# Hash attention: the bits of a pair made one whole pair ahead, and GpSimd's indirect DMAs put in front of its bit DMAs

## The chip, the cores and the metric

The kernel runs on one core of one Trainium2 chip. The metric is the device time of one execution in microseconds (us). Before the change it is 787.45 us, the median of three runs (785.88 to 792.85). The engines are named as in the profile: PE multiplies matrices and PEld loads its weights, DVE is the vector engine, ACT the scalar engine (it computes the exponentials), POOL is GpSimd, and SP issues most DMAs. Each engine runs its own list of instructions in order; a DMA is issued by one of SP, ACT or POOL, in that engine's order.

## The reference

Two parts follow each other. The first is attention in which a query sees only the keys of its own bucket; the bucket is made of the signs of six projections. With B = 4, H = 8, S = 768 and D = 64 there are 32 heads. The second is a mixer: an MLP over tokens and an MLP over channels.

```python
def _attn_ref(q, k, v, proj) -> np.ndarray:
    B, H, S, D = q.shape
    scale = 1.0 / np.sqrt(D)
    n_bits = proj.shape[1]
    q_bits = (np.einsum('bhsd,dk->bhsk', q, proj) > 0).astype(np.int64)
    k_bits = (np.einsum('bhsd,dk->bhsk', k, proj) > 0).astype(np.int64)
    powers = 2 ** np.arange(n_bits)
    q_bucket = np.sum(q_bits * powers, axis=-1)
    k_bucket = np.sum(k_bits * powers, axis=-1)
    mask = q_bucket[:, :, :, None] == k_bucket[:, :, None, :]
    scores = scale * np.matmul(q, k.transpose(0, 1, 3, 2))
    scores = np.where(mask, scores, -1000000000.0)
    scores = scores - np.max(scores, axis=-1, keepdims=True)
    attn = np.exp(scores)
    attn = attn / (np.sum(attn, axis=-1, keepdims=True) + 1e-09)
    return np.matmul(attn, v).astype(np.float32)
...
def _moe_ref(x, w_tok1, w_tok2, w_ch1, w_ch2) -> np.ndarray:
    xt = x.transpose(0, 2, 1)
    h = np.maximum(xt @ w_tok1, 0.0) @ w_tok2
    u = x + h.transpose(0, 2, 1)
    h2 = np.maximum(u @ w_ch1, 0.0) @ w_ch2
    return (u + h2).astype(np.float32)
```

## The kernel before

Two heads make a pair, so there are 16 pairs. Fourteen of them ("regular", `NREG = 14`, the loop `for n in range(NREG)` at L998 to L1061) compute whole 768 x 768 score matrices, with the bucket comparison added as a product of bits: a row of signs of the queries times a row of large values of the keys. The other two ("sorted", `class Sorted`, pairs 14 and 15) put queries and keys into tables ordered by bucket and compute only blocks within a bucket; their work is spread over the iterations of the regular pairs. After the attention, from about 304 us on, the two MLPs run; they are not touched.

One iteration of the loop handles regular pair n. On PE it holds, in order:

- the scores of pair n (`scores`, L484 to L518): 12 blocks of 128 keys by 384 queries for two heads. Each block is a product of bits (`sc<-bits`) and two products of q and k (`sc<-qk`), all at L501. ACT turns each block into exponentials (`exps<-sc`, L412), DVE adds them up (`esd`, L448 to L457).
- the sums of the pair before (`sums`, L534), and the projection of the next pair's q and k, `Hash` (L348 and L353), both into one PSUM tile called `hash`
- the weighing of pair n (`weigh`, L468) in two halves, exponentials times v into `acc`. ACT moves each half out as `num` (L477 and L478).

PSUM is handed out as a ring of four tiles with the tag "sc" (`bank_pair`, L269): a score block, the `hash` tile and the `acc` tile each take the next one, and a tile is taken anew only when its last reader has finished. A late reader of any of the four so holds up PE some blocks on.

`Hash.spread` (L358 to L377) makes the bits: two DVE comparisons (L364 for k, L365 for q) write signs into a corner of `XT`, and 16 small DMAs copy them into one of two tiles, `bitrows[n % 2]` (names `bits_119` and `bits_120` in the order of instructions): eight for k, of which SP issues six and ACT two, and eight for q, of which POOL issues six and SP two. In iteration n this is done for pair n + 1. `load_qk` (L272) brings q and k of a pair into one of three buffers; in iteration n it is called for pair n + 2, just ahead of the weighing.

The work of the sorted pairs hangs on a table of points in the loop (`todo`, `at`, `now_at`; L938 to L973). `SORTED` gives each sorted pair three iterations (first, made, back): 14 has (1, 6, 9) and 15 has (5, 10, 11). In iteration first its own q and k, loaded by `Sorted.load` into a buffer of the same three as `qk`, are hashed and counted. In the iterations first + 1, first + 2 and first + 3, at the point "loads" (ahead of the weighing in the text of the program), POOL issues eight indirect DMAs each time (`scatter`, L789), which write rows to the tables in DRAM. `put_bits` (L742) puts bits into these rows on ACT first. `fetch` reads the tables back, at the point "bits" of iteration made - 1. In the iterations back and back + 1 POOL issues six indirect DMAs each (`gather`, L909), which bring the result back; `store` follows. So indirect DMAs are issued in iterations 2, 3, 4, 6, 7, 8 (scatter) and 9, 10, 11, 12 (gather).

The weights of the MLPs are converted meanwhile by DVE and ACT (`Conversion`: lines around L177 to L206), a part in each iteration except 2 and 13.

## Time and profile before

| | us |
|---|---|
| runs before (median; lowest, highest) | 787.45; 785.88, 792.85 |
| the profiled execution, its own time | 783.04 |
| its span in the trace | 781.3 |

The profiled execution is 4.41 us below the median of the three runs, and 1.7 us of its time lie outside the span. The page shows the granted clock of TensorE at the full value in all 40 slices. Two parts of the page that the later text doesn't repeat show how the work lies in time: each character is the busy share of one fortieth of the span (19.5 us), in tenths. The attention is the first fifteen or sixteen characters.

```profile
DVE  5997898988979887999796889999899799889884
ACT  5676777667778755333313235656674666675331
POOL 2316661636643550011121000010000011000001
```

POOL is busy where it issues bit DMAs and indirect DMAs. Engines are named in the rows below by the part that a row is about: "SPq", "ACTq" are the issue of DMAs on those engines' queues. A row of the timeline has a start in us, a duration in us, the engine, the line, the operation, what it writes and reads, a count of instructions that the row groups, and in brackets the idle time before it and what ended it.

### The profile page before, as it was taken

The numbers are of one execution on the slowest core, as the hardware profiler recorded it, in microseconds if no ns is written. First come the engines' busy times: TensorE is split into PE (matmuls) and PEld (weight loads), VectorE is DVE, ScalarE is ACT, GpSimd is POOL, SyncE is SP. The second block draws the span as 40 slices with busy tenths as digits, with TensorE's granted clock in tenths as the row PEclk, the third lists the DMA queues.
The fourth block names the chain that finished last, engine by engine and source line by source line (L and its number), as shares of the span: only waits on it lengthen the run. The fifth ranks groups of instructions, "written<-read, shape, count | busy, mean of one in ns | idle before, by whom it ended". The sixth has DMA issues, their size and how long they took to land.

```text
span 781.3 us, 14554 instructions
## 1 busy us (share of the span) xinstructions
PE 771.9 (99%) x5549; PEld 520.1 (67%) x5549; DVE 675.2 (86%) x965; ACT 445.0 (57%) x826; POOL 175.1 (22%) x226
## 2 busy tenths in 40 slices
PE   9999999999999999999999999999999999999997
PEld 4555565557557654455544458888877888886886
DVE  5997898988979887999796889999899799889884
ACT  5676777667778755333313235656674666675331
POOL 2316661636643550011121000010000011000001
PEclk9999999999999999999999999999999999999999
DMA  7555477644677439897597997898666686850565
GB/s 252 210 193 150 147 225 222 217 110 164 174 206 212 149 62 231 270 264 140 101 266 235 310 394 268 251 283 215 219 212 212 236 246 135 251 156 3 198 162 129
DMA packets 131210, 157.80 MB, mean 202 GB/s; under 512 B 56000, under 2 KB 99520, under 8 KB 129216
## 3 DMA queue, kind: packets, MB, share of 16 engines
q1 hardware_dynamic: 119664, 136.29, 55.0%
q0 software_dynamic: 10768, 20.20, 12.8%
q8 instruction: 45, 0.74, 0.4%
q10 hardware_dynamic: 704, 0.33, 0.1%
q14 instruction: 29, 0.24, 0.1%
HBM read 107.71 MB, written 40.67 MB: 190 GB/s over the span
## 4 chain that ended last, share of the span: by engine, by line
PE 84%; DVE 9%; SPq 2%; DMA 2%; issue 1%; ACT 1%; another core or an unknown queue 0%; DVEq 0%; ACTq 0%
PE b L1323 50%; PE sc L501 14%; PE acc L468 12%; PE sc L423 1%; PE hash L534 1%; SPq L919 1%; DVE size L196 1%; PE ss L847 1%; DVE unit L195 1%; PE sacc L873 1%; DMA XT<-second 1%; DVE second L206 1%; DVE size L191 1%; PE ssums L861 1%; PE hash L353 1%
## 5 line engine op out<-in xcount | busy, mean ns | idle before, releaser
L412 ACT ACTIVATE exps<-sc 128x768 f32<-128x768 f32 (+1 forms) x181 | 126.1, 769 | 16.4 <-PE sc L501 12.4
L1323 PE MATMUL b<-R,second 128*128 128x256 f32 (+1 forms) x522 | 131.8, 408 | 0.0
L501 PE MATMUL sc<-qk 32*128 32x384 f32 (+1 forms) x1352 | 131.0, 458 | 0.3
L1323 PEld LDWEIGHTS b<-R,second 128*128 128x128 f32 x522 | 99.1, 190 | 28.5 <-issue 16.5
L468 PE MATMUL acc<-exps,vn 128*32 128x385 f32 (+1 forms) x1344 | 111.9, 486 | 0.0
L501 PEld LDWEIGHTS sc<-qk 32*128 32x128 f32 x1352 | 96.4, 185 | 17.1 <-issue 4.6
L468 PEld LDWEIGHTS acc<-exps,vn 128*32 128x32 f32 x1344 | 47.4, 109 | 58.0 <-issue 55.9
L1329 ACT COPY c<-b 128x256 f32<-128x256 f32 (+1 forms) x96 | 40.3, 426 | 79.3 <-PE b L1323 66.1
L457 DVE TENSOR_TENSOR esd<-esd,exps 128x768 f32<-128x768 f32 x70 | 67.0, 957 | 4.3
L789 POOL DMA_INDIRECT table<-XT,sorting x48 | 60.6, 1262 | 22.7 <-issue 11.7
L377 POOL DMA_DIRECT2D bits<-XT x78 | 38.9, 504 | 119.3 <-PE acc L468 47.2
L1323 PE MATMUL b<-XT,WC 128*128 128x256 f32 (+1 forms) x208 | 61.0, 428 | 0.0
L501 PE MATMUL sc<-bits 32*128 32x384 bf16 (+1 forms) x338 | 50.3, 311 | 1.5 <-ACT x L880 0.3
L2033 POOL DMA_DIRECT2D out<-second x7 | 8.5, 1213 | 186.8 <-DVE second L2027 81.5
L1323 PEld LDWEIGHTS b<-XT,WC 128*128 128x128 f32 x208 | 39.5, 190 | 15.4 <-issue 10.3
L1323 PE MATMUL b<-XT,SW 128*128 128x256 f32 (+1 forms) x164 | 47.0, 410 | 0.0
L453 DVE TENSOR_TENSOR esd<-esd,exps 128x768 f32<-128x768 f32 x42 | 40.3, 959 | 5.1 <-ACT exps L412 0.8
L1196 PE MATMUL t<-x,W 128*128 128x512 f32 x96 | 42.1, 594 | 0.3 <-DMA x<-bounced 0.3
L555 ACT COPY rec<-rec 32x384 f32<-32x384 f32 x56 | 28.5, 510 | 20.1 <-DVE rec L549 15.3
L1323 PEld LDWEIGHTS b<-XT,SW 128*128 128x128 f32 x164 | 31.1, 190 | 9.4 <-issue 4.1
L1196 PEld LDWEIGHTS t<-x,W 128*128 128x128 f32 x96 | 18.1, 190 | 23.3 <-issue 21.7
L448 DVE SCALAR_TENSOR_TENSOR esd<-exps 128x768 f32<-128x768 f32 x28 | 26.6, 949 | 7.6 <-ACT exps L412 5.6
(330 smaller groups left out, 1444.9 us busy)
## 6 DMA issues: line engine op xcount, KB each, us to landing
second<-left SPq DMA_DIRECT2D x20, 768.0 KB
qk<-in_qk_rows SPq DMA_DIRECT2D x13, 1152.0 KB
raw<-in_moe_w_ch SPq DMA_DIRECT2D x16, 768.0 KB
second<-left SPq DMA_DIRECT2D x18, 576.0 KB
WC<-hidden_left SPq DMA_DIRECT2D x18, 448.0 KB
x<-bounced SPq DMA_DIRECT2D x4, 1536.0 KB
XT<-second POOLq DMA_DIRECT2D x8, 768.0 KB
seen<-in_qk SPq DMA_DIRECT2D x15, 384.0 KB
```

What stands on the lines that cost most here:

```text
L377: queue.dma_start(out=to[at : at + 2 * BITS, half[j]], in_=g[of : of + 2 * BITS])
L412: return nc.scalar.activation(e[:, :, columns], sc, ACT.Exp, scale=SCALE)
L448: nc.vector.scalar_tensor_tensor(self.d, es[0], NR * EPS, es[1], op0=ALU.add, op1=ALU.add,)
L453: nc.vector.tensor_tensor(self.d, self.d, e, op=ALU.add)
L457: nc.vector.tensor_tensor(self.d, self.d, e, op=ALU.add)
L468: made = nc.tensor.matmul(acc[D * i + d : D * i + d + 32], vn[:, i, c, d : d + 32], e[:, i], start=(c == 0), stop=(c == NR - 1),)
L501: nc.tensor.matmul(made[j, piece][:, i], k[at : at + 32, ks], q[at : at + 32], start=part < 0, stop=part == 1,)
L555: nc.scalar.copy(rec[other : other + 32, h], rec[at : at + 32, h])
L789: nc.gpsimd.indirect_dma_start(out=tables[2 * w + i], out_offset=bass.IndirectOffsetOnAxis(ap=self.at[:, x : x + 1], axis=0), in_=row, in_ ...
L1196: nc.tensor.matmul(ps, W1[:, r, P * j : P * j + P], x[:, r], start=(r == 0), stop=(r == NR - 1),)
L1323: nc.tensor.matmul(ps, left(k), right(k), start=start and k == ks[0], stop=stop and k == ks[-1], skip_group_check=True,)
L1329: nc.scalar.copy(c, ps)
```

## The change

It does the following.

1. SP issues the two k-bit DMAs of each pair that ACT issued.
2. `Sorted.load` writes into a part of `WC1` and no longer into one of the three `qk` buffers.
3. `put_bits` runs on POOL, at the beginning of iteration first + 1, and no longer on ACT.
4. `scatter` and `gather` move to a new point "scored", right after the scores of pair n in the text of the program. Ahead of them POOL copies one element of the last exponential (`scored`, a tile of 1 x 1 x 1), so that they start only when that exponential is there. They so stand ahead of the iteration's bit DMAs on POOL, where before they stood behind them.
5. `fetch` moves to the beginning of iteration made - 1.
6. `load_qk(n + 3)` is called right after the scores of pair n, where `load_qk(n + 2)` was called further down; `load_qk(2)` is called in iteration 0 ahead of `Hash(1)`, and `load_qk(3)` at the place of the old call there.
7. In iteration n the bits of pair n + 2 are made, those of n + 1 no longer. An extra `Hash(2)` stands at the end of iteration 0, and iteration 12 makes none.

```diff
@@ -369,8 +369,7 @@
                 for j in range(2):
                     for i in range(4):
                         at, of = 32 * i, 32 * j + BITS * i
-                        queue = nc.scalar if j and i > 1 else nc.sync
-                        queue.dma_start(out=to[at : at + BITS, S:][:, quarter[j]], in_=g[of : of + BITS, : HALF // 2])
+                        nc.sync.dma_start(out=to[at : at + BITS, S:][:, quarter[j]], in_=g[of : of + BITS, : HALF // 2])
                     for i in range(4):
                         at, of = 32 * i, D + 32 * j + 2 * BITS * (i % 2)
                         queue = nc.sync if j and i > 1 else nc.gpsimd
@@ -674,7 +673,7 @@
                 self.e = [[exps[:, 4 + NG * k + g, :, :SLOTS] for g in range(NG)] for k in range(2)]
 
             def load(self):
-                self.t = pool.tile([P, 2 * (S + HALF)], F32, name="qk", tag="qk", bufs=3)
+                self.t = flat(WC1[:, 1:3])[:, : 2 * (S + HALF)]
                 nc.sync.dma_start(out=self.t, in_=sorted_qkv[self.which])
 
             def load_rows(self):
@@ -739,7 +738,7 @@
                 bits = copy[:, :BW].rearrange("p (r w i c) -> p r w i c", w=2, i=2, c=CW)
                 for to, r in ((rows_q, 0), (rows_kv[0], 0), (rows_kv[1], NR - 1)):
                     width, count = to.shape[3], to.shape[1]
-                    nc.scalar.copy(
+                    nc.gpsimd.tensor_copy(
                         to[:, :, :, width - 4 :], bits[:, r : r + count, int(width == KW), :, :4],
                     )
 
@@ -955,18 +954,17 @@
             at(first, "last", call("load_rows"))
             at(first, "weighed", call("turn_bits"), call("own_groups"))
             at(first, "end", call("count"))
-            at(first + 1, "begin", call("places"), call("numbers"))
-            at(first + 1, "loads", call("put_bits"))
+            at(first + 1, "begin", call("places"), call("numbers"), call("put_bits"))
             for n in range(3):
-                at(first + 1 + n, "loads", call("scatter", 8))
-            at(made - 1, "bits", call("fetch"))
+                at(first + 1 + n, "scored", call("scatter", 8))
+            at(made - 1, "begin", call("fetch"))
             at(made - 1, "last", call("turn_q"))
             at(made, "sums", call("copy_bits"))
             at(made, "newton", call("turn_k"), call("turn_sorted_bits"))
             at(made, "end", call("scores", 0), call("scores", 1), call("weigh"))
             at(made, "last", call("divide"), call("turn_back"))
-            at(back, "loads", call("gather", range(NR // 2)))
-            at(back + 1, "loads", call("gather", range(NR // 2, NR)))
+            at(back, "scored", call("gather", range(NR // 2)))
+            at(back + 1, "scored", call("gather", range(NR // 2, NR)))
             at(back + 2, "begin", call("store"))
         at(0, "loads", prepare_sorting)
         at(NREG - 1, "begin", fetch_turned)
@@ -979,6 +977,7 @@
         nc.gpsimd.memset(exps[:, :, :, HALF:], -EPS)
         load_qk(1)
         constants = prepare_bits()
+        scored = pool.tile([1, 1, 1], F32, name="scored", tag="scored", bufs=1)
 
         opening = bank_pair("opening")
         for _ in range(6):
@@ -1002,6 +1001,10 @@
                 load_v(n + 1)
                 now_at(n, "begin")
                 scores(halves)
+                load_qk(n + 3)
+                if (n, "scored") in todo:
+                    nc.gpsimd.tensor_copy(scored, halves[1].es[-1][:1, :1, :1])
+                    now_at(n, "scored")
                 hashing = bank_pair("hash")
                 halves[0].add()
                 halves[0].add_last()
@@ -1011,6 +1014,7 @@
                     now.first_scores()
                     if now.half:
                         hashing = bank_pair("hash")
+                        load_qk(2)
                         Hash(1, hashing[:, 1], "sums").spread()
                         break
                     now.add()
@@ -1019,8 +1023,8 @@
             halves[1].add()
             if before:
                 before.sums(hashing[:, 0])
-            if 0 < n < NREG - 1:
-                Hash(n + 1, hashing[:, 1], f"sums{n - 1}").spread()
+            if 0 < n < NREG - 2:
+                Hash(n + 2, hashing[:, 1], f"sums{n - 1}").spread()
             acc = bank_pair("acc")
             now_at(n, "hash")
             now_at(n, "sums")
@@ -1033,7 +1037,7 @@
                 halves[1].add_last()
             if n == 0:
                 load_v(1)
-            load_qk(n + 2)
+                load_qk(3)
             now_at(n, "bits")
             now_at(n, "loads")
             if converts:
@@ -1054,6 +1058,8 @@
             if converts:
                 weights.turnover()
             halves[1].weigh(acc)
+            if n == 0:
+                Hash(2, hashing[:, 0], "sums").spread()
             now_at(n, "end")
             if n and n % 2 == 0:
                 bounce(pool.tile([P, 2 * S], F32, name="stage", tag="stage", bufs=1), n - 2)
```

The next rows show how this moves instructions on three engines. A row has the line, the operation, what it writes and reads (`sc`, `hash`, `acc` are PSUM tiles; `bits_119` and `bits_120` are the two bit tiles; `table_123` to `table_126` are the sorted tables), the shape, and what it waits for: the name of an engine, or of one of the DMA queues' semaphores (DMAHW for SP and ACT, DMASW for POOL). Lines are those of each kernel's own text.

On POOL, in iteration 2, the first with indirect DMAs. Before, where the last two bit DMAs of that iteration stand in front (they go to `bits_120`, the tile of pair 3):

```order
L377 DMA bits_120<-XT 16x384 [waits DMASW0_49,PE_49]
L377 DMA bits_120<-XT 16x384 [waits DMASW1_49,PE_49]
L789 DMA table_123<-XT,sorting 1792x68 [waits DMAHW7_49,DMASW2_49,Activation_49]
L789 DMA table_124<-XT,sorting 1792x68 [waits DMAHW0_49,DMASW3_49]
L789 DMA table_125<-XT,sorting 1792x132 [waits DMAHW0_49,DMAHW1_49,DMASW4_49,Activation_49]
L789 DMA table_126<-XT,sorting 1792x132 [waits DMAHW2_49,DMASW5_49]
```

After, from the last copy of `put_bits` to the first bit DMAs of the same iteration (they go to `bits_119`, the tile of pair 4):

```order
L741 COPY XT<-sorting 128x2x4 [waits DMAHW4_49]
L1006 COPY scored<-exps 1x1 [waits Activation_49]
L788 DMA table_123<-XT,sorting 1792x68 [waits DMASW2_49,DMAHW7_49,DVE_49,Pool_49]
L788 DMA table_124<-XT,sorting 1792x68 [waits DMAHW0_49,DMASW3_49]
L788 DMA table_125<-XT,sorting 1792x132 [waits DMAHW1_49,DMASW4_49,Pool_49]
L788 DMA table_126<-XT,sorting 1792x132 [waits DMASW5_49]
L788 DMA table_123<-XT,sorting 1792x68 [waits DMASW6_49,DMASW2_49]
L788 DMA table_124<-XT,sorting 1792x68 [waits DMASW7_49,DMASW3_49]
L788 DMA table_125<-XT,sorting 1792x132 [waits DMASW4_49,DMASW0_49]
L788 DMA table_126<-XT,sorting 1792x132 [waits DMASW5_49,DMASW1_49]
L376 DMA bits_119<-XT 16x384 [waits DVE_49,PE_49]
L376 DMA bits_119<-XT 16x384 [waits PE_49] x3
```

The copies of `put_bits` (three, of which the last is shown) and the copy `scored` come new; the indirect DMAs behind them wait for the last exponential through `scored`, and the bit DMAs of the iteration now follow the eighth of them.

On DVE, from the conversion of weights in iteration 0 to the first comparisons of iteration 1. Before:

```order
L196 TENSOR_TENSOR size<-size,unit 128x768 [waits DVE_49]
L206 SCALAR_TENSOR_TENSOR W_108<-raw,size 128x768 [waits DVE_49]
L448 SCALAR_TENSOR_TENSOR esd<-exps 128x768 [waits Activation_49]
L453 TENSOR_TENSOR esd<-esd,exps 128x768 [waits DVE_49,Activation_49] x2
L457 TENSOR_TENSOR esd<-esd,exps 128x768 [waits DVE_49,Activation_49] x2
L448 SCALAR_TENSOR_TENSOR esd<-exps 128x768 [waits Activation_49]
L453 TENSOR_TENSOR esd<-esd,exps 128x768 [waits DVE_49,Activation_49]
L364 TENSOR_SCALAR XT<-hash 64x192 [waits PE_49]
L365 TENSOR_SCALAR XT<-hash 64x384
```

After:

```order
L196 TENSOR_TENSOR size<-size,unit 128x768 [waits DVE_49]
L206 SCALAR_TENSOR_TENSOR W_108<-raw,size 128x768 [waits DVE_49]
L364 TENSOR_SCALAR XT<-hash 64x192 [waits PE_49]
L365 TENSOR_SCALAR XT<-hash 64x384
L447 SCALAR_TENSOR_TENSOR esd<-exps 128x768 [waits Activation_49]
L452 TENSOR_TENSOR esd<-esd,exps 128x768 [waits DVE_49,Activation_49] x2
L456 TENSOR_TENSOR esd<-esd,exps 128x768 [waits DVE_49,Activation_49] x2
L447 SCALAR_TENSOR_TENSOR esd<-exps 128x768 [waits Activation_49]
L452 TENSOR_TENSOR esd<-esd,exps 128x768 [waits DVE_49,Activation_49]
```

The two comparisons of `Hash(2)` now follow `L206`, the last step of the conversion of iteration 0; they stood behind the adds of iteration 1 before.

On PE, the first scores of pair 1, from the second half of the first key block on. Before:

```order
L501 LDWEIGHTS bits_120 [waits DVE_49]
L501 MATMUL sc<-bits_120 128x192 [waits PE_49]
L501 LDWEIGHTS bits_120
L501 MATMUL sc<-bits_120 128x192
L501 MATMUL sc<-qk 128x192 x4
L501 LDWEIGHTS bits_120 [waits DMAHW1_49]
L501 MATMUL sc<-bits_120 128x384 [waits Activation_49]
L501 LDWEIGHTS bits_120 [waits DMAHW2_49]
L501 MATMUL sc<-bits_120 128x384
```

After:

```order
L500 LDWEIGHTS bits_120
L500 MATMUL sc<-bits_120 128x192 [waits Activation_49]
L500 LDWEIGHTS bits_120
L500 MATMUL sc<-bits_120 128x192
L500 MATMUL sc<-qk 128x192 x4
L500 LDWEIGHTS bits_120 [waits DVE_49,DMAHW0_49]
L500 MATMUL sc<-bits_120 128x384 [waits PE_49]
L500 LDWEIGHTS bits_120 [waits DMAHW1_49]
L500 MATMUL sc<-bits_120 128x384
```

The third block (a product of 128x384 after the four 128x192 rows) takes a PSUM tile that in the new order held the projections of `Hash(2)`; its first weight load waits for DVE, where it waited before for a DMA of bits alone.

## Prediction

> **What bounds the kernel now.** I read the page first.
>
> ```profile
> PE 771.9 (99%) x5549; PEld 520.1 (67%) x5549; DVE 675.2 (86%) x965; ACT 445.0 (57%) x826; POOL 175.1 (22%) x226
> PE 84%; DVE 9%; SPq 2%; DMA 2%; issue 1%; ACT 1%; another core or an unknown queue 0%; DVEq 0%; ACTq 0%
> ```
>
> PE looks busy all the time, and the chain of work that ended last runs mostly over it. But a busy share of 99% says nothing here: the ends of matmuls are modelled. So I asked a second view, the windows, for the same piece of work in all pairs: from the first to the last score product of a pair, pairs 1 to 13 in order. Columns: window and its length, then busy time (and instructions) of PE, PEld, DVE, ACT and POOL, granted clock, DMA share, GB/s.
>
> ```profile
> 26.41:35.57 9.16, 9.16 (x134) 7.06 (x138) 8.64 (x19) 8.36 (x13) 0.54 (x3) 1.00 1.01 384
> 46.25:55.41 9.16, 9.16 (x135) 7.06 (x138) 8.64 (x21) 8.37 (x15) 0.00 (x0) 1.00 0.95 380
> 64.60:77.67 13.07, 12.87 (x134) 8.78 (x138) 8.35 (x10) 8.48 (x13) 8.65 (x8) 1.00 0.77 211
> 86.85:96.01 9.16, 9.16 (x134) 7.08 (x138) 8.45 (x10) 8.36 (x13) 6.95 (x6) 1.00 0.71 278
> 105.20:115.17 9.97, 9.88 (x134) 8.03 (x138) 9.52 (x12) 8.56 (x13) 5.90 (x6) 1.00 0.99 356
> 125.86:135.02 9.16, 9.16 (x134) 7.08 (x138) 7.50 (x20) 8.37 (x15) 0.00 (x0) 1.00 1.02 260
> 154.77:165.72 10.95, 10.39 (x130) 7.68 (x126) 9.15 (x12) 9.55 (x16) 1.92 (x2) 1.00 0.78 172
> 174.90:184.48 9.58, 9.45 (x135) 7.62 (x138) 8.62 (x11) 7.31 (x11) 7.04 (x7) 1.00 0.69 269
> 193.86:204.65 10.79, 10.58 (x134) 7.90 (x138) 10.24 (x12) 8.20 (x13) 7.47 (x6) 1.00 0.91 264
> 213.84:224.61 10.77, 10.77 (x134) 8.32 (x138) 6.93 (x9) 8.38 (x13) 4.94 (x5) 1.00 1.02 262
> 243.95:253.42 9.47, 9.38 (x134) 7.62 (x134) 8.39 (x11) 9.19 (x16) 0.00 (x0) 1.00 0.92 194
> 262.60:272.76 10.16, 10.08 (x135) 8.19 (x138) 8.53 (x10) 8.34 (x13) 5.75 (x5) 1.00 0.69 249
> 281.95:294.82 12.87, 12.49 (x134) 8.66 (x138) 10.33 (x13) 8.48 (x13) 4.94 (x5) 1.00 0.58 122
> sum 134.27, PE 132.53 PEld 101.08 DVE 113.30 ACT 109.95 POOL 54.10; mean PE 10.19 PEld 7.78 DVE 8.71 ACT 8.46 POOL 4.16
> ```
>
> The same products take 9.16 us in four pairs and up to 13.07 in the others, at a granted clock of 1.00 throughout. The losses against 9.16 are, for pairs 3, 5, 7, 8 and 9: 3.91, 0.81, 1.79, 0.42, 1.63, together 8.56; for pairs 10 to 13: 1.61, 0.31, 1.00, 3.71, together 6.63. The sum is 134.27 - 13 x 9.16 = 15.19 us. That is all that this change can win in the scores. The slow pairs are those whose preceding iteration had indirect DMAs (2, 3, 4, 6 to 12); of these only pair 4 is clean. Pairs 1, 2 and 6, behind an iteration without them, are clean.
>
> The ACT rows of the timeline show how a slow pair begins.
>
> ```profile
> 67.17 0.49 ACT L412 ACTIVATE exps<-sc 128x384 f32<-128x384 f32 x1 [1.93 <-PE sc L501]
> 106.39 0.58 ACT L478 ACTIVATE num<-acc,vsum 128x384 f32<-128x384 f32 x1 [2.92 <-PE sc L501]
> 284.22 0.58 ACT L478 ACTIVATE num<-acc,vsum 128x384 f32<-128x384 f32 x1 [4.00 <-PE sc L501]
> 285.75 0.49 ACT L412 ACTIVATE exps<-sc 128x384 f32<-128x384 f32 x1 [0.95 <-PE sc L501]
> ```
>
> Pair 3 gets its first exponential at 67.17, 2.57 us after its scores began at 64.60; pair 13 at 285.75, 3.80 after 281.95. In pairs 5 and 13 ACT also gets the second half of the weighing late (106.39 and 284.22, after idle times of 2.92 and 4.00 us). Late exponentials hold the ring of four PSUM tiles, and PE pays. What delays PE there, no row says; what stands beside it is POOL and the queues.
>
> ```profile
> 99.18 3.09 POOL L377 DMA_DIRECT2D bits<-XT  x6 [1.29 <-DVE rec L547]
> 102.57 1.44 POOL L789 DMA_INDIRECT table<-XT,sorting  x1 [0.30 <-issue]
> ...
> 116.88 0.97 POOL L789 DMA_INDIRECT table<-XT,sorting  x1 [0.30 <-issue]
> L789 POOL DMA_INDIRECT table<-XT,sorting x48 | 60.6, 1262 | 22.7 <-issue 11.7 <-DMA table<-XT,sorting 9.9 <-ACT XT L742 0.5
> L909 POOL DMA_INDIRECT XT<-result,sorting x24 | 30.0, 1250 | 7.7 <-issue 6.8 <-DMA bits<-XT 1.0
> 97.92 4.31 SPq L373 DMA_DIRECT2D bits<-XT  x6
> 102.33 1.17 SPq L377 DMA_DIRECT2D bits<-XT  x2
> ```
>
> Ahead of pair 5 (its scores begin at 105.20) POOL issues six bit DMAs to 102.27, then eight indirect ones from 102.57 to 117.85, right across the change from weighing to scores. SP's last bit DMA is issued at 103.50, 1.70 us before the scores that need it.
>
> **The change part by part.**
>
> *Indirect DMAs moved ahead (point "scored").* They now start when the last exponential ends.
>
> ```profile
> 93.53 3.81 ACT L412 ACTIVATE exps<-sc 128x768 f32<-128x768 f32 x5
> ```
>
> In pair 4 that is 97.34 instead of 102.57. One costs 1.26 busy and 0.30 issue, 1.56 us. Eight end at 97.34 + 12.5 = 109.8 or later (DMA waits of 9.9 us over 48 add 1.7 to a burst); six gathers at 106.7. The scores begin at 105.20, so of eight scatters about three still run behind it, of six gathers one. If the loss goes with what still runs there, 8.56 x 3/8 = 3.2 and 6.63 x 1/6 = 1.1 stay, 4.3 us, and 15.2 - 4.3 = 10.9 go. The bounds: all 15.2 goes, or none, or the loss grows, since the whole burst now also lies in the weighing. I take 10.9 because pair 4, with 6.95 us of POOL in its scores, shows that indirect DMAs away from the change of phase cost nothing.
>
> *POOL's bit DMAs behind them* start at about 110 to 112 and take 3.09: to 115. They are for pair n + 2, whose scores began in iteration 6 at 125.86. Ten us of cover; without the pair ahead they would have been 10 us late. Cost nothing.
>
> *ACT without DMAs and `put_bits`.*
>
> ```profile
> 59.35 1.33 ACTq L373 DMA_DIRECT2D bits<-XT  x2
> 61.13 2.14 ACT L555 COPY rec<-rec 32x384 f32<-32x384 f32 x4 [3.54 <-DMA bits<-XT]
> 63.30 0.46 ACT L742 COPY XT<-sorting 128x48 f32<-128x48 f32 x3
> ```
>
> ACT loses 1.33 us of issue per pair, once a wait of 3.54 and twice 0.46. None of it lies on PE's path except ahead of pair 3 (and 7, the other `put_bits`), where ACT reaches its first exponential late anyway; that is inside the 15.2 counted above, so I add nothing. On POOL the three copies stand where it is idle (between 0.5 and, each at an indirect DMA's 1.26, 3.8 us), ahead of the wait for the exponential; cover: the whole of the scores, 9.16.
>
> *SP with two more DMAs a pair.* One costs 4.31/6 = 0.72, so 1.4 us a pair. With bits a pair ahead the cover is an iteration; what is late next is `load_qk`, but that is now issued ahead of the bits, a pair and a half before its use. `fetch`, moved to the beginning of iterations 5 and 9, waits on SP for the last scatters (about 112) with `load_qk(8)` queued behind it; pair 8's q and k are hashed only in iteration 6. Nothing, bounded by one late load, a few us. `Sorted.load` in another place: nothing.
>
> *`Hash(2)` at the end of iteration 0.* This is a new stall, and the order shows it: its comparisons stand on DVE behind the conversion's L206, and the third score block of pair 1 takes their PSUM tile.
>
> ```profile
> 96.61 0.33 PE L348 MATMUL hash<-qk,projs 128*32 128x192 f32 x2
> ...
> 97.26 1.15 PE L468 MATMUL acc<-exps,vn 128*32 128x385 f32 x12
> ...
> 27.81 0.32 PE L501 MATMUL sc<-bits 32*128 32x384 bf16 x2
> ...
> 31.11 0.96 DVE L206 SCALAR_TENSOR_TENSOR W<-raw,size 128x768 uint32<-128x768 uint32 x1
> 18.74 0.35 DVE L364 TENSOR_SCALAR XT<-hash 64x192 bf16<-64x192 f32 x1 [1.22 <-PE hash L348]
> 19.12 0.56 DVE L365 TENSOR_SCALAR XT<-hash 64x384 bf16<-64x384 f32 x1
> ```
>
> DVE ends L206 at 32.07 and the comparisons at 32.07 + 0.35 + 0.56 = 32.98. A hash takes PE 97.26 - 96.61 = 0.65 (the two PE rows of pair 4), and PE began that block at 27.81, so it would now reach it at 28.46. So PE stands 4.5 us. Pair 1 was clean, so nothing pays it back. SP's two more DMAs and `load_qk(2)` ahead of pair 1's bits (about 2.0 us later than before) fall inside these 4.5. The hash itself is not extra: iteration 12 makes none.
>
> *Sum.* 783.04 + 4.5 - 10.9 = 776.6 for the profiled execution. It lies 4.41 under the median, so 781.0 by the median.
>
> One rule speaks against bursts in the weighing. DVE adds exponentials there, and the row of such adds is this:
>
> ```profile
> L453 DVE TENSOR_TENSOR esd<-esd,exps x42: 957/959/961, 12.9 to 294.7; 128x768 f32<-128x768 f32 x42
> ```
>
> Shortest, median and longest are 957, 959 and 961 ns, in scores with indirect DMAs and without. The Trainium skill ("SBUF — State Buffer", section "SBUF: two separate sides") says that DVE and GpSimd share a port pair as a lock, which an operation of DVE with two SBUF inputs can lose to a GpSimd operation that reads SBUF, for all of its length; PE and ACT never wait for a port. By that rule DVE would be held up, as in the last rival. The trace doesn't agree: no add is longer.
>
> **The rivals.**
>
> *A. Everything goes.* If PE's delay comes from bits, queues or ACT's DMAs, the bits a pair ahead remove it whole: 783.04 + 4.5 - 15.2 = 772.3, by the median 776.8. For it: SP's last bits are issued 1.70 us before their use. Against: pair 4 is clean with the same bits, and in the view of waits no row of PE or PEld names a DMA of bits.
>
> *B. The loss moves (slower).* The burst itself delays the second half of the weighing, wherever it runs (ACT's waits at 106.39 and 284.22 speak for it), and it still crosses the change of phase everywhere. Then all 15.2 stay: 783.04 + 4.5 = 787.5, by the median 792.0. It decides if less than 4.5 of the 15.2 goes. Against: the gathers end only 1.5 us behind the change of phase.
>
> *C. DVE becomes late.* Each of ten bursts now runs for 8 us beside DVE's work in the weighing. If each step of DVE there with two inputs, some five an iteration (the adds, the Newton steps, the division), waits half an indirect DMA, 0.63 us, DVE is 3.1 us later. In the windows it is idle for 134.27 - 113.30 = 21.0 us, 1.6 a pair, so 1.5 remain, 15 us over ten iterations: 783.04 + 4.5 - 10.9 + 15 = 791.6, by the median 796, and 807 if the old losses stay too. That is the mechanism of the rule named above. The L453 row speaks against it.
>
> *D. The change does less than it says.* If the last exponential comes late itself, as in pair 3, the bursts move little. That is B's time less 0 to 4.
>
> **How the numbers follow.** The forecast, part of the loss gone, has 0.42, with a range of its own of 778 to 786; A has 0.30 (776.8); B and D 0.19 (788 to 792); C 0.09 (796 to 807). The range from 775 to 793 leaves out C and thin ends of A and B, about 0.2. About 1% is what a measurement of this kernel can tell from no change, 7.9 us: faster means below 779.6, which is nearly all of A and a fifth of the forecast's, 0.36; slower means above 795.3, C and the end of B, 0.12; the rest, 0.52, is the same.
>
> **What would show it.** In the changed kernel's timeline: a gap or a stretched product on PE in pair 1 near 28.5, to the end of DVE's comparisons near 33 (without it the 4.5 is wrong). The first L788 of each burst right at the end of the last exponential. No DMA issue on ACT. The windows of pairs 10 to 13 near 9.4 and of pairs 3 to 9 near 9.8: all at 9.16 is A, unchanged ones are B, and longer weighings with late `num` are B or C. If indirect DMAs do not cause the losses at all, the forecast fails, for the division by what still runs behind the change of phase rests on that.

## The result, and the profile after

| | before | after |
|---|---|---|
| runs shown with the result, us (median; lowest, highest) | 790.73; 785.88, 792.85 | 818.66; 811.82, 819.42 |
| ratio after to before, 95% interval | | 1.0351 [1.0302, 1.0400] |
| profiled execution, us (span) | 783.04 (781.3) | 811.82 (810.1) |
| the two kernels once more, on other runs (r1): ratio | | 1.0017 [1.0002, 1.0031] |

The changed kernel was 3.5% slower in the runs with the result, and level (0.2% slower) in a later set. Both numbers are right, and the difference between them is the main finding below. The forecast was 781.0 with a range of 775 to 793.

The page of the changed kernel still shows a busy PE and a chain of work that runs over it:

```profile
PE 789.0 (97%) x5549; PEld 521.9 (64%) x5549; DVE 675.3 (83%) x965; ACT 444.4 (55%) x820; POOL 178.4 (22%) x242
PE 95%; DVE 2%; issue 1%; ACT 1%; POOL 1%; DMA 0%; SPq 0%; DVEq 0%; POOLq 0%
```

To see where the 28.8 us between the two profiled executions lie, the windows view is asked for five stretches of the attention: iteration 1, iterations 2 to 5, iteration 6 (with the scores of the first sorted pair), iterations 7 to 10 (10 holds those of the second), and iterations 11 to 13 up to the first product of the token MLP. Columns as in the prediction. The kernel before:

```profile
26.34:46.19 19.85, 19.85 (x272) 11.61 (x269) 18.85 (x35) 15.46 (x26) 3.51 (x9) 1.00 0.57 207
46.19:125.79 79.60, 79.31 (x1005) 46.52 (x1006) 70.53 (x101) 57.47 (x99) 42.23 (x48) 1.00 0.58 189
125.79:154.40 28.61, 28.43 (x408) 18.09 (x408) 26.01 (x45) 20.99 (x42) 11.17 (x12) 1.00 0.77 246
154.40:243.81 89.41, 88.51 (x1145) 57.81 (x1146) 78.08 (x100) 63.53 (x109) 49.45 (x55) 1.00 0.59 170
243.81:304.01 60.20, 59.64 (x736) 35.34 (x735) 51.08 (x64) 42.99 (x73) 20.55 (x24) 1.00 0.58 139
```

The changed kernel, the same five:

```profile
27.07:54.35 27.28, 22.81 (x270) 14.12 (x267) 21.32 (x37) 14.91 (x26) 5.82 (x12) 0.87 0.58 199
54.35:140.54 86.19, 83.98 (x1005) 48.27 (x1006) 68.92 (x99) 56.84 (x96) 43.63 (x54) 1.00 0.59 175
140.54:172.56 32.02, 31.23 (x407) 17.34 (x406) 25.66 (x45) 20.68 (x39) 13.31 (x18) 1.00 0.64 207
172.56:269.49 96.93, 94.55 (x1146) 56.03 (x1146) 78.13 (x100) 63.45 (x109) 48.43 (x57) 1.00 0.56 158
269.49:331.96 62.47, 58.43 (x724) 34.12 (x723) 51.27 (x64) 45.81 (x78) 18.71 (x20) 1.00 0.50 107
```

The second number of a row is its length. Iteration 1 is 7.43 us longer, iterations 2 to 5 6.59, iteration 6 3.41, iterations 7 to 10 7.52, the rest 2.27. With 0.73 for the later start (the hash moved to iteration 0) that is 27.95 of the 28.8; the MLPs behind take 0.8 more. No stretch came out shorter.

**Iteration 1.** The rows of the timeline, PE and DVE of the changed kernel, and the granted clock in windows of the same place:

```profile
33.24 0.50 PE L500 MATMUL sc<-bits 32*128 32x384 bf16 x2 [4.47 <-DVE XT L365]
32.53 0.56 DVE L365 TENSOR_SCALAR XT<-hash 64x384 bf16<-64x384 f32 x1
```

```profile
27.07:33.24 6.17, 1.70 (x34) 1.36 (x31) 5.91 (x16) 1.76 (x4) 0.00 (x0) 0.90 0.88 297
33.24:36.72 3.48, 3.48 (x26) 3.01 (x30) 0.84 (x1) 0.38 (x1) 2.90 (x6) 0.50 0.99 373
36.72:38.88 2.16, 2.16 (x19) 1.77 (x17) 1.59 (x2) 1.13 (x2) 0.00 (x0) 0.52 0.65 216
38.88:43.73 4.85, 4.85 (x68) 3.49 (x66) 3.33 (x5) 4.64 (x7) 0.00 (x0) 1.00 0.18 38
```

PE waits 4.47 us for the comparisons, which end at 33.09; 4.5 was forecast. But then it runs for 5.64 us (33.24 to 38.88) at a granted clock of 0.50 to 0.52, and loses nearly 3 us more: 7.43 in all. The windows put the half clock at 31.97 to 38.79, 6.8 us; in the trace of r1 below, the same kernel, it lasts 3.4 us (32.24 to 35.64) behind a wait of 3.94. The Trainium skill ("TensorE: Matmul & The Clock Gate", section "Part 1: The HAM clock gate (the "warmup" mystery)") says that an idle PE falls to half its clock and needs some 3.4 us of sustained work to be released; the trace agrees with the half, and here it took some 5.6 us.

**Iteration 2, the first with a burst** (the indirect DMAs of one iteration, eight or six). Rows of the timeline of the changed kernel: products of the weighing, two of its groups of weight loads, ACT's second half of it, and one of POOL's indirect DMAs of that time:

```profile
64.83 6.32 PE L467 MATMUL acc<-exps,vn 128*32 128x385 f32 x72
71.34 2.13 PE L467 MATMUL acc<-exps,vn 128*32 128x384 f32 x9 [0.19 <-issue]
71.36 0.15 PEld L467 LDWEIGHTS acc<-exps,vn 128*32 128x32 f32 x4 [0.90 <-issue]
72.11 0.16 PEld L467 LDWEIGHTS acc<-exps,vn 128*32 128x32 f32 x4 [0.60 <-issue]
```

```profile
78.93 0.58 ACT L477 ACTIVATE num<-acc,vsum 128x384 f32<-128x384 f32 x1 [6.01 <-PE acc L467]
```

```profile
71.84 0.97 POOL L788 DMA_INDIRECT table<-XT,sorting  x1 [0.30 <-issue]
```

A weighing is 96 products, 24 groups of four, and takes 7.9 us elsewhere, 0.33 a group; this one takes 14.06 (64.83 to 78.89). The first 72 products run at nearly that rate, though the burst of eight, from 65.79 to 76.63, has begun. The last 24 take 7.5 us: from 71.36 on weight loads come 0.7 to 1.6 us apart, four at first (71.36, 72.11), later often a single one, until 2 us behind the burst's end. The wait is put down to "issue": PE waited for nothing that the profile shows, at a granted clock of 1.00.

The next iteration is another case. The windows of the two weighings, and the scores behind the second:

```profile
64.83:78.82 13.99, 11.79 (x102) 3.41 (x92) 8.27 (x12) 3.66 (x8) 11.25 (x14) 1.00 0.58 158
89.30:97.28 7.98, 7.98 (x102) 3.73 (x93) 7.46 (x11) 4.63 (x9) 6.54 (x6) 1.00 0.44 165
97.35:109.75 12.40, 12.40 (x134) 8.46 (x138) 8.27 (x9) 8.30 (x13) 6.92 (x9) 1.00 0.39 120
```

POOL's burst of iteration 3 begins at 89.69, and the weighing beside it loses nothing; the scores that follow take 12.40 us in place of 9.16. So in these two iterations PE slows 5 and 8 us behind the start of the burst, once in the weighing and once in the scores.

**The end of the attention.**

Two rows of the changed kernel, then one of the kernel before:

```profile
324.17 4.05 PE L467 MATMUL acc<-exps,vn 128*32 128x384 f32 x48
331.96 2.59 PE L1202 MATMUL t<-x,W 128*128 128x512 f32 x3 [3.74 <-ACT num L477]
```

```profile
304.01 8.42 PE L1196 MATMUL t<-x,W 128*128 128x512 f32 x19
```

The first product of the token MLP waits 3.74 us for ACT's last `num`. Before, it began at 304.01 straight behind the last weighing. Argued from the text of the program, not shown: the number of tiles taken from the ring of four is the same in both kernels, but the order in which they come free is not, since `Hash(2)` holds one longer, and the MLP's first tile now lies where the last `acc` was. In s1 below, one more tile taken from the ring ends the wait.

### The profile page after: what moved, and what is told of

Same layout as the page of the kernel before. It is cut to its first block, busy times and chain, and to the rows that moved or that the text cites. A ratio compares the mean times of both kernels' runs of the same rounds, so it can differ in the third digit from the quotient of the medians.

```text
span 810.1 us, 14582 instructions
## 1 busy us (share of the span) xinstructions
PE 789.0 (97%) x5549; PEld 521.9 (64%) x5549; DVE 675.3 (83%) x965; ACT 444.4 (55%) x820; POOL 178.4 (22%) x242
## 4 chain that ended last, share of the span: by engine, by line
PE 95%; DVE 2%; issue 1%; ACT 1%; POOL 1%; DMA 0%; SPq 0%; DVEq 0%; POOLq 0%
PE b L1329 49%; PE sc L500 16%; PE acc L467 13%; PE t L1202 5%; PE t L1242 4%; PE sc L422 1%; PE hash L533 1%; PE sacc L872 1%; PE ss L846 1%; PE ssums L860 1%; PE hash L348 1%; PE hash L353 0%; POOL bits L376 0%; ACT rec L554 0%; DMA qk<-in_qk 0%
## 5 line engine op out<-in xcount | busy, mean ns | idle before, releaser
L467 PE MATMUL acc<-exps,vn 128*32 128x385 f32 (+1 forms) x1344 | 124.7, 486 | 4.3 <-issue 4.3
L500 PEld LDWEIGHTS sc<-qk 32*128 32x128 f32 x1352 | 98.5, 188 | 20.4 <-issue 10.4
L1335 ACT COPY c<-b 128x256 f32<-128x256 f32 (+1 forms) x96 | 40.3, 426 | 79.4 <-PE b L1329 69.4
L788 POOL DMA_INDIRECT table<-XT,sorting x48 | 60.2, 1254 | 14.7 <-issue 11.7
L500 PE MATMUL sc<-bits 32*128 32x384 bf16 (+1 forms) x338 | 52.0, 315 | 4.6 <-DVE XT L365 4.5
L376 POOL DMA_DIRECT2D bits<-XT x78 | 38.7, 507 | 38.7 <-DVE XT L365 21.4
L452 DVE TENSOR_TENSOR esd<-esd,exps 128x768 f32<-128x768 f32 x42 | 40.3, 958 | 7.9 <-ACT exps L411 3.7
L447 DVE SCALAR_TENSOR_TENSOR esd<-exps 128x768 f32<-128x768 f32 x28 | 26.6, 951 | 20.2 <-ACT exps L411 19.7
L477 ACT ACTIVATE num<-acc,vsum 128x384 f32<-128x384 f32 x28 | 16.3, 581 | 44.0 <-PE acc L467 19.7
```

What stands on the lines that cost most here:

```text
L376: queue.dma_start(out=to[at : at + 2 * BITS, half[j]], in_=g[of : of + 2 * BITS])
L452: nc.vector.tensor_tensor(self.d, self.d, e, op=ALU.add)
L467: made = nc.tensor.matmul(acc[D * i + d : D * i + d + 32], vn[:, i, c, d : d + 32], e[:, i], start=(c == 0), stop=(c == NR - 1),)
L500: nc.tensor.matmul(made[j, piece][:, i], k[at : at + 32, ks], q[at : at + 32], start=part < 0, stop=part == 1,)
L788: nc.gpsimd.indirect_dma_start(out=tables[2 * w + i], out_offset=bass.IndirectOffsetOnAxis(ap=self.at[:, x : x + 1], axis=0), in_=row, in_ ...
L1335: nc.scalar.copy(c, ps)
```

## The experiments

All kernels of a set ran on one chip, beside the kernel before; a `diff` below shows the main part of an edit, not all of it. The sets fall into two kinds by what the kernel before takes: 786.0 to 791.0 us (the result, and sets 1, 4 and 5), called lossy here, and 777.2 to 778.1 (sets 2 and 3), called clean. Times are medians.

| set, before | kernel | us | ratio, 95% interval |
|---|---|---|---|
| 1, 790.97 | e1 after, no indirect DMAs | 779.25 | 0.9854 [0.9773, 0.9934] |
| | e2 before, no indirect DMAs | 774.05 | 0.9806 [0.9723, 0.9889] |
| | e3 after, indirect DMAs behind bits | 817.25 | 1.0329 [1.0241, 1.0417] |
| | e4 after, conversion behind Hash(2) | 811.22 | 1.0271 [1.0185, 1.0358] |
| 2, 777.20 | e5 after, indirect DMAs and load back | 796.46 | 1.0250 [1.0218, 1.0283] |
| | e6 before, load early | 772.09 | 0.9943 [0.9922, 0.9964] |
| | e7 after, load back | 795.37 | 1.0212 [1.0171, 1.0253] |
| | e8 before, indirect DMAs at "scored" | 871.14 | 1.1173 [1.1111, 1.1235] |
| 3, 778.08 | r1 after | 778.56 | 1.0017 [1.0002, 1.0031] |
| | r2 before | 777.85 | 1.0004 [0.9988, 1.0021] |
| | r3 as e5 | 795.62 | 1.0228 [1.0198, 1.0258] |
| | r4 as e6 | 773.02 | 0.9941 [0.9916, 0.9967] |
| 4, 786.03 | s1 after, two mends | 804.97 | 1.0236 [1.0204, 1.0269] |
| | s2 after, fetch late | 810.85 | 1.0341 [1.0294, 1.0388] |
| | s3 as e6 | 793.49 | 1.0095 [1.0064, 1.0126] |
| 5, 790.29 | t1 as e5 | 815.09 | 1.0304 [1.0223, 1.0386] |
| | t2 as s1 | 807.66 | 1.0194 [1.0117, 1.0271] |
| | t3 before, plain DMAs for indirect ones | 778.86 | 0.9839 [0.9770, 0.9908] |

### Are the indirect DMAs the cause? (e1, e2, t3)

```diff
-                    nc.gpsimd.indirect_dma_start(
-                        out=tables[2 * w + i],
-                        out_offset=bass.IndirectOffsetOnAxis(ap=self.at[:, x : x + 1], axis=0),
-                        in_=row, in_offset=None,
-                    )
```

The six indirect DMAs of each `gather` go too, and one memset stands for what they brought. e1, from the changed kernel:

> The changed kernel with all 72 indirect DMAs left out (scatter and gather issue none, a memset stands for the gathered result), so the two sorted pairs are not computed from their own tables. Theory: PE is slowed for as long as POOL works through a burst of indirect DMAs, wherever the burst lies; the stages from iteration 2 on lose about 33 us to it in the changed kernel, and these go: about 779 beside the profiled 811.8 (about 785 by the median). Pair 1 keeps its 7.4 us and the end of the attention its 3.7. Rival: the loss comes from the other parts (ten bit DMAs on SP, bits behind, queues), then the time stays above 805.

e2, from the kernel before:

> The kernel before with the same 72 indirect DMAs left out. Theory: the 15.2 us that its scores lose against 9.16 us go, about 768 beside the profiled 783.0 (773 to 776 by the median). Rival (bits that land late are the cause): the losses stay and the time is within 1% of the kernel before.

The thirteen score stretches of each (as in the prediction), their sum row, e1 and then e2:

```profile
sum 126.86, PE 122.87 PEld 95.78 DVE 111.77 ACT 109.89 POOL 3.87; mean PE 9.45 PEld 7.37 DVE 8.60 ACT 8.45 POOL 0.30
```

```profile
sum 119.72, PE 119.66 PEld 93.00 DVE 105.71 ACT 110.36 POOL 0.50; mean PE 9.20 PEld 7.15 DVE 8.13 ACT 8.49 POOL 0.04
```

Before, this sum was 134.27. In e2 it is 119.72, which is 9.16 for every pair but the two behind a sorted one (9.48 each). In e1 only pair 1 is longer still, by 7.16. So the losses go with the indirect DMAs, all but the 0.6 us of the two pairs behind a sorted one, and the cost of these DMAs can be read from whole times in the lossy sets: 790.97 - 774.05 = 16.9 us before, 818.66 - 779.25 = 39.4 in the changed kernel (818.66 is from the runs with the result, the others from set 1).

t3 keeps the place, the bytes and the engine, and takes away the indirect addressing (`gather` likewise); the rows then go to the tables in order and not by bucket:

```diff
+                    nc.gpsimd.dma_start(out=tables[2 * w + i][P * r : P * r + P], in_=row)
```

> The kernel before with each of the 72 indirect DMAs replaced by a plain DMA of the same bytes on POOL, to and from rows in order (the sorted pairs' tables are then not in bucket order and those two pairs come out otherwise). On a chip with losses: if the indirect addressing causes them, 774 as without any (e2 against 791 there) and scores of 9.23; if any small DMA that POOL issues there does, 785 to 791 as before. On a chip without losses: 778, nothing told.

```profile
sum 119.70, PE 119.65 PEld 93.00 DVE 103.05 ACT 110.34 POOL 15.37; mean PE 9.20 PEld 7.15 DVE 7.93 ACT 8.49 POOL 1.18
```

No score stretch loses anything, in a lossy set: it is the indirect form that costs PE, not every transfer of POOL at that place. In the view of groups, one issue of t3 costs POOL 563 ns, one of the changed kernel 1254:

```profile
L789 POOL DMA_DIRECT2D table<-XT x48 | 26.7, 563 | 1.2 <-issue 0.6 <-ACT XT L742 0.5
```

```profile
L788 POOL DMA_INDIRECT table<-XT,sorting x48 | 60.2, 1254 | 14.7 <-issue 11.7 <-DVE XT L558 1.2 <-DVE XT L364 0.6
```

So a burst of plain DMAs is also less than half as long. The addressing itself, POOL's longer work for it and the scattered rows were not taken apart. t3 is 4.8 us above e2, in other sets.

### Is it the place of the bursts, or what stands beside them? (e3, e5, e6, e7, e8)

e3 puts only the point of `scatter` and `gather` back (`gather`'s two lines likewise):

```diff
-                at(first + 1 + n, "scored", call("scatter", 8))
+                at(first + 1 + n, "loads", call("scatter", 8))
```

> The changed kernel with only the point of scatter and gather put back (point loads, behind the bit DMAs, no copy of the last exponential); bits still a pair ahead. Theory: the bursts cost what they cost before, about 15 us instead of 33, so about 794 profiled (800 by the median). Rival (the bits a pair ahead or SP's ten DMAs are what costs): it stays at 812 to 819.

817.25, a ratio of 1.0329 [1.0241, 1.0417] beside the changed kernel's 1.0351: no difference that can be measured. The point that the prediction argued with is not what costs.

e5 is e3 with the load of q and k at its old place too; e7 has the load alone put back; e6 is the kernel before with the load alone moved:

```diff
                 scores(halves)
+                load_qk(n + 2)
```

> As e3 (indirect DMAs behind the bits again), and the load of q and k put back behind the bits too (load_qk(n + 3) at the place where load_qk(n + 2) stood); bits still a pair ahead. e1 and e2 put the cost of the 72 indirect DMAs at 39 us in the changed kernel and 17 before. Theory L: a burst costs PE more when the big load of q and k no longer runs beside it; then the cost falls back to 17 and the time to 779 + 17 = 796. Theory H: the bits a pair ahead raise it; then it stays near e3's 817.

> The kernel before with one thing changed: load_qk(n + 2) is called right after the scores of pair n, no longer behind the bits. Theory L: the cost of the indirect DMAs rises from 17 to about 40, 774 + 40 = 814. Theory H (and every theory in which the load's place is indifferent): 787 to 791 as before.

> The changed kernel with only the load of q and k put back behind the bits. Theory L: the burst now runs in the weighing ahead of the load, without it beside, so the cost stays near 39 and the time near 818. Theory H: about 818 too. A theory in which the load itself, early in the weighing, slows PE: about 795.

This set was the first clean one: no scores lose anything to the bursts in e5, e6 or e7, so it tells nothing of what raises their cost. The 18 to 19 us of e5 and e7 have other causes. Pair 1 and the end of the attention they share with every form of the changed kernel; their own cause is shown by PE in iteration 6 of e5:

```profile
142.59 0.53 PE L348 MATMUL hash<-qk,projs 128*32 128x192 f32 x1 [5.21 <-DMA qk<-in_qk_rows]
```

A hash two pairs ahead needs q and k two pairs ahead; behind the bits and `fetch` on SP they come 5.21 us late, and 4.46 us late in iteration 10. So the early load belongs to the bits a pair ahead. Alone, in e6, it wins 0.6% in a clean set.

e8 moves only the bursts, with bits still for the next pair:

> The kernel before with only scatter and gather moved to the point scored, behind the copy of the last exponential (put_bits goes to POOL with them); bits for the next pair behind them on POOL. The bits then start some 12 us late in ten iterations and land after the scores should begin: about 5 us a time, 50 in all, less what the waiting PE no longer loses to the burst (up to 17): 820 to 840. If the bits are hidden all the same: 775 to 795.

871.14, worse than the 820 to 840 expected: without the bits a pair ahead the bits do come too late behind a burst. In e8's trace PE waits for them eight times ahead of the scores, 66.7 us in all and first 10.59 us at 76.22, and the mean granted clock falls to 0.95.

### The same kernels in a clean and in a lossy set (r1 to r4, s3, t1)

> The changed kernel unchanged, beside the kernel before on one chip. On the chip of e5 to e8 no stage of e5, e6 and e7 loses anything to indirect DMAs (all scores 9.23), while on the chip of e1 to e4 they cost 17 to 41 us. If the cost hangs on the chip: on a chip where the kernel before takes 775 to 780, the changed kernel takes 779 to 783 (e1's 779 without indirect DMAs is its floor); on one where before takes 785 to 793, it takes 812 to 819. If the cost hangs on the kernel: 3.5% slower on both.

> The kernel before unchanged, for its trace on this chip. If the chip decides: all scores 9.23 where it takes 775 to 780, 15 us of losses where it takes 785 to 793.

The score stretches of r1 (pair 1, pair 3, and the sum), the sum of the lossy trace of the same kernel, and the stretches of r2 (pair 3 and the sum):

```profile
26.08:41.10 15.02, 11.08 (x134) 8.68 (x138) 11.10 (x16) 7.85 (x12) 2.90 (x6) 0.89 0.70 254
...
70.13:79.29 9.16, 9.16 (x134) 7.08 (x138) 6.32 (x8) 8.36 (x13) 6.69 (x10) 1.00 0.78 161
...
sum 125.57, PE 121.58 PEld 94.58 DVE 112.07 ACT 109.83 POOL 55.48; mean PE 9.35 PEld 7.28 DVE 8.62 ACT 8.45 POOL 4.27
```

```profile
sum 138.74, PE 133.66 PEld 102.63 DVE 113.26 ACT 109.57 POOL 40.80; mean PE 10.28 PEld 7.89 DVE 8.71 ACT 8.43 POOL 3.14
```

```profile
64.18:73.34 9.16, 9.16 (x134) 7.07 (x138) 8.34 (x10) 8.36 (x13) 5.92 (x6) 1.00 0.89 245
...
sum 119.75, PE 119.67 PEld 92.98 DVE 105.14 ACT 110.40 POOL 51.65; mean PE 9.21 PEld 7.15 DVE 8.09 ACT 8.49 POOL 3.97
```

The kernel before, unchanged, has the sum of e2, though POOL is busy with indirect DMAs for 5.92 us inside the scores of pair 3. The 15 us that the prediction set out to win do not exist here. For the changed kernel the lossy trace is 33.9 us longer than r1's (spans 810.1 and 776.2); 138.74 - 125.57 = 13.2 of them lie in the scores, most of the rest in what PE does between the scores of one pair and the next. POOL's own work is the same in both kinds: a scatter takes 1263 ns in r1, 1254 in the lossy trace.

```profile
L788 POOL DMA_INDIRECT table<-XT,sorting x48 | 60.6, 1263 | 14.7 <-issue 12.0 <-DVE XT L558 1.2 <-DVE XT L364 0.6
```

So whether an indirect DMA slows PE depends on something outside the program. What it is stays open. The record numbers the chips of sets 1 to 5 as 15, 5, 6, 1 and 5: number 5 stands at a clean set (2) and at a lossy one (5). If that is one chip both times, the chip alone does not decide it.

r3 and r4 repeat e5 and e6:

> e5 again. On a chip with losses, theory L (the place of the load of q and k decides what a burst costs) gives about 796 against e3's 817 on such a chip; if the load's place is indifferent to the bursts, about 817 + 13 for the late loads of pairs 8 and 12 that e5 showed.

> e6 again (before, with the load of q and k right after the scores). On a chip with losses: theory L about 814, indifferent 787 to 791. On a chip without: 772 again, 0.6% less than the kernel before.

Both as in set 2 (1.0228 and 0.9941), since the set was clean again. The lossy sets 4 and 5 answered:

> The kernel before with the load of q and k right after the scores, once more. Without losses 772 to 773 beside 778 for the kernel before, as twice already. On a chip with losses: 814 if the load's place is what raises the cost of a burst, 787 to 791 if not.

> e5 again (the changed kernel with indirect DMAs and load of q and k behind the bits). On a chip with losses: if the early load is what raises the cost, the scores lose about 15 us as before, and the time is before's plus 19 (what e5 was above before on the chip without losses), about 805; if the bits a pair ahead raise it too, 25 or more are lost and it takes 815 or more. On a chip without losses: 796 again.

The row of pair 3 in s3, and the sum rows of s3 and of t1:

```profile
64.49:81.79 17.30, 16.68 (x134) 10.89 (x138) 9.24 (x10) 9.16 (x13) 8.74 (x8) 0.80 0.61 163
...
sum 146.34, PE 143.18 PEld 106.61 DVE 120.50 ACT 112.01 POOL 54.81; mean PE 11.01 PEld 8.20 DVE 9.27 ACT 8.62 POOL 4.22
```

```profile
sum 148.15, PE 138.85 PEld 104.27 DVE 118.69 ACT 109.45 POOL 55.49; mean PE 10.68 PEld 8.02 DVE 9.13 ACT 8.42 POOL 4.27
```

In s3 the early load alone raises the loss from 15 to 146.34 - 119.7 = 26.6 us. Part of the rise is the clock's: in three of the pairs the granted clock is at half for a time, in pair 3 from 72.6 to 79.4 (the row's mean is 0.80), where the kernel before has 1.00 in all thirteen; 13.6 us at half the clock in all cost some 6.8 (an estimate: half of them). In whole times, against the kernel before of the same set, the early load takes a ratio of 0.994 in the clean sets to 1.0095 in the lossy one, 1.5 points. The whole change goes from 1.0017 to 1.0351, 3.3 points. So the early load alone explains about half of what was missing.

t1, with load and bursts at their old places and bits a pair ahead, loses 148.15 - 119.7 - 7.1 (pair 1) = 21.4 us in these stretches and takes 815.09 in all, against the 805 expected of a load that alone decides. That looks like a second part at work, but it is not shown: t1's ratio of 1.0304 [1.0223, 1.0386] is not clear of the 1.0250 [1.0218, 1.0283] that the same kernel has in a clean set. And e3, which differs from t1 in the early load alone, has 1.0329, though it has none of the late loads, which in clean sets take the changed kernel from 1.0017 to 1.0212 and 1.0250 (e7, e5). So the early load is the part that is seen to raise the cost of a burst in the kernel before, and points the same way in the changed kernel, where e3 was not run in a clean set. Why it does, and whether bits or bursts add to it, stays open.

### The two new stalls, and the fetch (e4, s1, t2, s2)

e4 and s1 put the conversion of iteration 0 behind the comparisons; s1 also takes one spare tile of the ring, with a product of 32 x 32 that nothing reads (the last part of s1's edit):

```diff
             if n == 0:
                 Hash(2, hashing[:, 0], "sums").spread()
+                nc.tensor.matmul(bank_pair("spare")[:32, 0, :32], ones, ones, start=True, stop=True)
+                weights.join()
+                weights.turnover()
```

> The changed kernel with the weight conversion of iteration 0 behind the comparisons of Hash(2) on DVE. Theory: the stall of pair 1 falls from 4.5 us to under 1 and the slow products behind it (about 2.5 us) go with it: 6 to 7 us less, about 805 profiled (812 by the median). Rival (the time is lost elsewhere in pair 1 and paid anyway): no difference.

> The changed kernel with e4's order (conversion of iteration 0 behind the comparisons of Hash(2)) and one spare PSUM tile of the ring taken in iteration 0 (a product of 32 x 32 fills it), so that the first tile of the token MLP is no longer the one of the last acc. Where indirect DMAs cost nothing: 778.6 - 5.1 (pair 1 from 5.9 to 0.8 of loss) - 3.7 (end of the attention) = 769.8, 1.1% under the kernel before. If these two are not additive (the attention's end is set by something else): 773 to 779. On a chip with losses: 818 - 11 = 807.

> s1 again (the changed kernel with pair 1 and the attention's end mended). On a chip without losses 769 to 771, 1% under the kernel before at 778. On a chip with losses 805 as before.

PE in e4, at the block that waited 4.47 us, and in s1 at the first product of the MLP:

```profile
28.63 0.34 PE L500 MATMUL sc<-bits 32*128 32x384 bf16 x2 [0.59 <-DVE XT L365]
```

```profile
326.18 4.13 PE L1206 MATMUL t<-x,W 128*128 128x512 f32 x9
```

The first stall falls from 4.47 to 0.59 us and no slow clock follows; the second is gone. e4 takes 811.22, 7.4 less than the changed kernel's median in other runs; its ratio, 1.0271 [1.0185, 1.0358], is not clear of 1.0351. s1 and t2 take 1.0236 and 1.0194 times the kernel before, where the changed kernel takes 1.0351. Both sets were lossy, so the 769.8 us that these mends should give in a clean one are an estimate and were not seen.

s2 puts `fetch` back to its old point:

> The changed kernel with fetch put back to the point bits of iteration made - 1. Where indirect DMAs cost nothing: the blocks around the two sorted pairs, 18.7 us in the changed kernel and 21.4 and 23.6 before, go back by 2.7 + 4.9 = 7.6: 786. If they were long for another reason (store, loads): 778.6 as the changed kernel. On a chip with losses: 818 to 826.

810.85 in a lossy set, a ratio of 1.0341: nothing to be told apart from the changed kernel, where 818 to 826 was expected. The clean traces have to serve instead. Iterations 6 and 7 to 10 take 30.64 and 88.20 us in r2 and 27.94 and 83.30 in r1:

```profile
120.65:151.29 30.64, 28.02 (x408) 17.85 (x409) 26.74 (x46) 20.99 (x42) 10.69 (x12) 1.00 0.74 243
151.29:239.49 88.20, 84.75 (x1146) 50.46 (x1146) 77.94 (x100) 63.80 (x109) 51.89 (x55) 0.98 0.61 173
```

```profile
126.60:154.54 27.94, 27.94 (x407) 17.71 (x406) 26.40 (x45) 20.45 (x39) 9.07 (x11) 1.00 0.66 225
154.54:237.84 83.30, 83.27 (x1146) 50.52 (x1146) 77.39 (x100) 63.65 (x109) 53.42 (x63) 1.00 0.66 185
```

In r2 DVE waits for the fetched table, its adds of the iteration are late, and the sorted pair's scores then wait for DVE:

```profile
214.13 0.71 DVE L819 STREAM_TRANSPOSE x<-XT 128x512 f32<-128x512 f32 x1 [3.57 <-DMA XT<-table]
```

```profile
228.47 5.77 PE L847 MATMUL ss<-x 32*128 32x256 bf16 x80 [3.42 <-DVE x L832]
```

r1 has neither wait. The gain of 2.70 + 4.90 = 7.6 us pays for pair 1 (15.02 - 9.16 = 5.86) there, and with the 3.74 at the end the two kernels come out even. But it is not the fetch's alone. e6 has `fetch` at its old point and only the load early; the same two stretches in its trace:

```profile
121.02:149.88 28.86, 28.02 (x409) 17.80 (x409) 26.68 (x46) 20.98 (x42) 11.04 (x12) 1.00 0.71 223
149.88:234.27 84.39, 83.65 (x1145) 50.83 (x1144) 78.07 (x101) 63.82 (x109) 51.44 (x55) 1.00 0.63 180
```

With the load early the table of the late fetch holds DVE up for 1.11 us there and no longer for 3.57, and 88.20 falls to 84.39; in r4, the same kernel, the two stretches are 31.49 and 84.18. So the early load alone brings most of the 4.9, and at most 2.0 to 4.4 of the 7.6 us are left for the fetch.

## Why the prediction was wrong

**The step that failed** is "I take 10.9 because pair 4, with 6.95 us of POOL in its scores, shows that indirect DMAs away from the change of phase cost nothing". One clean pair was made a rule of place. e3 shows that the place of the bursts decides nothing that can be measured (817.25 and 818.66); the weighing of iteration 2 lost 6.1 us, and in iteration 3 a burst that began as early still cost the scores behind it 3.2. Instead of 10.9 us less, the bursts cost 39.4 - 16.9 = 22.5 us more in the lossy sets, and in the clean ones there was nothing to win. The prediction did name a growing loss among its bounds, and gave it neither a price nor a chance.

**Two places of luck.** In the clean set the changed kernel takes 778.56, inside the range; but nothing was won in the scores there, and the time comes from stalls and gains most of which the prediction costed at nothing. And all that is not indirect DMAs was forecast at 4.5 us and measures 779.25 - 774.05 = 5.2 (e1 and e2); but this is some 11 us of stalls (pair 1 and the end of the attention) less what the early load and fetch won back.

**The cause was right, its reading too narrow.** Indirect DMAs are behind the 15.2 us (e2, all but 0.6), and only the indirect form (t3). The prediction took that cost as fixed by the kernel. r2 shows that it isn't.

**`Hash(2)`** was found at its place and sized right as a wait (4.5 forecast, 4.47 measured). The clock behind it was left out, 3 us in the lossy trace. "Pair 1 was clean, so nothing pays it back" held.

**POOL's bits behind the bursts cost nothing**: right. In r1 all pairs from 2 on are at the speed of e2 with these bits; e8 shows what they cost without the pair ahead.

**ACT without DMAs, SP with two more**: nothing, as said; no pair of r1 from 2 on is longer for either.

**`load_qk` early and `fetch` early** were both costed at nothing. The load is worth 0.6% in a clean set and costs 1.0% in a lossy one (e6, s3); the fetch is worth at most 2.0 to 4.4 us in the clean traces, and nothing that can be measured in a lossy set (s2).

**The end of the attention** was left out: 3.74 us, which one more tile of the ring removes (s1). In the changed kernel's trace it is a wait for ACT at the first product of the MLP, where the kernel before has none.

**The rivals.** B, that the burst delays the weighing wherever it runs, was the right direction, though not every weighing is delayed; its price (all 15.2 stay) was too low, since the loss grew. D didn't come: the first burst starts at 65.79, 1.0 us behind the last exponential. C, a late DVE, is refuted by the adds that now lie beside the bursts (none of those of the row in the prediction, now L452, does in the changed kernel). They are 30 of the 70 of another line, and the longest of the 30 takes 961 ns:

```profile
L456 DVE TENSOR_TENSOR esd<-esd,exps x70: 916/958/975, 15.6 to 322.0; 128x768 f32<-128x768 f32 x70
```

A, that everything goes, is what t3 gives, by another way: plain addresses. A's own mechanism (bits, queues, ACT's DMAs) is not borne out: the changed kernel has all three out of the way, and loses more.

## What to carry to other kernels

A loss that follows one kind of instruction is first measured by leaving that instruction out, in both kernels, before its place is argued over. A kernel is timed in more than one set before a saving of 2% is attributed to its code. Work moved ahead takes a PSUM tile with it: look through the order of instructions for every wait that changed its engine, at the far end of the ring too.

## What was not expected of the hardware

Indirect DMAs issued by GpSimd slowed PE in some sets and not in others, with the same program and the same time of POOL for each (1254 and 1263 ns). Where they did, the last 24 of 96 products of a weighing took 7.5 us in place of 2.0, at a granted clock of 1.00 and without any wait that the profile names; in two bursts the slow stretch began 5 and 8 us behind the first indirect DMA. Plain DMAs of the same bytes, 563 ns each, did not. After a wait of 4.47 us PE ran at half its clock for 5.64 us, and the half clock lasted 6.8 us in that trace and 3.4 in r1's.
